# An order of loads and of weight conversions at the start of an attention and gated-network kernel

## Chip, cores, metric

One core of one Trainium2 chip. The metric is the device time of one launch in microseconds, as the median of several runs. The five engines are TensorE (PE, with its weight loads shown apart as PEld), VectorE (DVE), ScalarE (ACT), GpSimd (POOL) and SyncE (SP), whose queue here issues nearly all transfers. Each engine takes its instructions strictly in program order.

## What is computed

Three stages follow each other. First attention with a causal window: 4 sequences of 576 tokens, 8 heads of 64 columns, the first four heads with a window of 32 neighbours, the others with every fourth token of 128. Then a gated layer, and at last a soft mixture of 8 experts over all 2304 tokens.

```python
scores = np.where(masks[None], scale * np.matmul(q, k.transpose(0, 1, 3, 2)), -1e9)
attn = np.exp(scores - scores.max(-1, keepdims=True))
attn = attn / (attn.sum(-1, keepdims=True) + 1e-09)
x = np.matmul(attn, v)                      # to 2304 x 512
x = (1 / (1 + np.exp(-(x @ w_gate)))) * (x @ w_val) @ w_out      # 512 -> 1536 -> 512
logits = x @ phi                            # 32 slots
d, c = softmax(logits, 0), softmax(logits, 1)
slots = d.T @ x                             # 8 experts x 4 slots
out = c @ experts(slots, w1, w2)            # relu between w1 and w2
```

## The kernel before

**Work and its names.** Tokens are cut into five blocks, n = 0 to 4 (four of 512 tokens, one of 256). The attention of one block is four *units*, one for each pair of heads, so units 0 to 3 belong to block 0, units 4 and on to the next. A unit loads its queries and keys (`qk`, line 273, 528 or 576 KB) and its values (`v`, line 280, 512 KB). TensorE makes the scores (`s_ps`, line 162) on top of a mask (line 148); VectorE takes the maximum (`mx`, 176) and subtracts it (178); ScalarE takes the exponential (184); VectorE sums it (`su`, 186), adds 1e-9 (187), inverts (188) and scales (189; from unit 4 on GpSimd does the scaling). TensorE transposes the shares (`tr`, 195), ScalarE copies them out (`pt_ring`, 196), TensorE weights the values with them (`xp`, 222), 32 products that the hardware runs as 64 passes. The result is split into a high part (`x_hi`, ScalarE, 250) and a remainder (`x_lo`, VectorE, 251).

**Weight tiles.** The gate and value weights are twelve *tiles* f = 0 to 11 of 128 columns each. They come as doubles (`st`, line 365, 1 MB) and are *converted* to single precision by integer work in two halves of 512 columns (`convert`, from line 371): a ScalarE step (383), two VectorE steps (384, 385), one GpSimd step (386). The converted tile is stored to DRAM for later (`wg`, 369) and *split* into a high and a low part (`split_w`: ScalarE 437, VectorE 438). `l1` multiplies a tile with block 0: for each half (a = 0 gate, a = 1 value) twelve products of 512 columns (line 474) into one of two PSUM banks (`l1ps`). ScalarE's tanh (484) empties the bank of the first half, VectorE's gate (`gated`, 460) that of the second; the bank is then free for the half after the next.

**Order.** The order in the program is written by emission, and an instruction scheduler of the framework sorts TensorE, VectorE, ScalarE and GpSimd between the points that are pinned; loads in this part are pinned in the order in which they are emitted (`ld`). The start runs block 0's attention (`s_step`, `t_step`, `p_step`), and `head` is the call that issues the first weight tile's load. Within these steps, after step `C0`, tile 0's conversion, the loads of units 4 and 5, and tile 1's conversion are emitted (lines 889 to 897). The loop behind takes tile f's split, then the conversion of tile f + 2 (`LA`), then `l1`, with the attention of the next blocks spread between.

**Buffers.** Values of two units share a buffer and there are two of them, so those of units 4 and 5 wait until unit 1 is weighted. Staged doubles (`l2`) have two buffers: tile 2's load waits until tile 0 has been converted.

Of the kernel before, what the change touches and what calls it, by code (L numbers as in the profile page):

```python
# [39 lines left out]
def k_cols(n, hp):  # L40
    if n < 4:
        return 544 if hp < 2 else 640
    return 640 if hp < 2 else 1024
# [13 lines left out]
def tile_kernel(  # L57
# [25 lines left out]
    def b8(tag, shape, dt, name):  # L83
        return big.tile(shape, dt, tag=tag, name=name, bufs=BUFS[tag])
# [23 lines left out]
    def keep_warm(count):  # L108
        for _ in range(count):
            nc.tensor.matmul(idle, lhsT=zero[:, 0:P], rhs=zero[:, 512:1024], start=True, stop=True)  # L110
# [61 lines left out]
    def softmax(u, norm):  # L172
        s = u["s"].rearrange("p (a c) -> p a c", a=8)
        mx = sm.tile([P, 8], F32, tag="mx", name="mx")
        for r in range(2):
            nc.vector.tensor_reduce(mx[:, 4 * r : 4 * r + 4], u["s_ps"][r], AX.X, ALU.max)  # L176
        for r in range(2):
            nc.vector.tensor_tensor(
                s[:, 4 * r : 4 * r + 4],
                u["s_ps"][r],  # L180
                mx[:, 4 * r : 4 * r + 4].unsqueeze(2).to_broadcast([P, 4, 64]),
                ALU.subtract,
            )
        nc.scalar.activation(s, s, AF.Exp, scale=0.125)
        su = sm.tile([P, 8], F32, tag="su", name="su")
        nc.vector.tensor_reduce(su, s, AX.X, ALU.add)
        nc.vector.tensor_scalar(su, su, 1e-9, None, ALU.add)
        nc.vector.reciprocal(su, su)
        norm.tensor_tensor(s, s, su.unsqueeze(2).to_broadcast([P, 8, 64]), ALU.mult)
# [66 lines left out]
    def ld(ins):  # L256
        return tc.keep_in_program_order(ins) if early[0] else ins

    def attn_steps(pbs, norm, head=None):
        jobs = [(n, hp) for n in pbs for hp in HP_ORDER]  # L260
        us = [{"id": j, "z": z} for z, j in enumerate(jobs)]
        tags = ["qk", "qk", "gb", "gb"] if head else ["qk"] * len(jobs)

        def load_qk(z):
            n, hp = jobs[z]
            w = 512 + k_cols(n, hp)
            us[z]["qk"] = b8(tags[z], [P, 2048], F32, "qk")
            if n < 4:
                us[z]["s"], us[z]["slot"] = sm4[:, HP_ORDER.index(hp)], z % 4
            else:  # L270
                us[z]["s"] = pt_ring[:, 2 + z % 2].rearrange("p c i q -> p (c i q)")
                us[z]["slot"] = z % 2
            ld(nc.sync.dma_start(us[z]["qk"][:, 0:w], qkv[n * NHP + hp, :, VCOLS : VCOLS + w]))

        def load_v(z):
            n, hp = jobs[z]
            if z % 2 == 0:
                v2 = b8("v", [P, 2, VCOLS], F32, "v2")
                us[z]["v"], us[z + 1]["v"] = v2[:, 0], v2[:, 1]
            ld(nc.sync.dma_start(us[z]["v"], qkv[n * NHP + hp, :, 0:VCOLS]))  # L280

        def load(z, what):
            if z < len(us) and not head:
                what(z)

        begun = []

        def first(what):
            if what not in begun:
                begun.append(what)  # L290
                what(0)
                what(1)

        def s_step(z, ts=range(4)):
            if z == 0 and 0 in ts:
                if head:
                    load_qk(0)
                    ld(nc.sync.dma_start(msk, masks.bitcast(BF16)))
                    load_qk(1)
                    ld(nc.sync.dma_start(cst, consts))  # L300
                    load_v(0)
                    load_qk(2)
                    load_v(1)
                    head()
                    load_qk(3)
                    load_v(2)
                    load_v(3)
                else:
                    first(load_qk)
                    first(load_v)  # L310
            scores(us[z], ts)
            if 3 not in ts:
                return
            if 2 <= z and not head:
                weighted(us[z - 2], range(2), us[z])
            softmax(us[z], norm)
            load(z + 2, load_qk)
            if z == 0:
                load(2, load_v)

        def t_step(z):
            turn_unit(us[z])

        def p_step(z, ts=range(2)):
            if head or z + 2 >= len(us):
                weighted(us[z], ts)
            if head:
                keep_warm(WP)
            if 1 in ts:
                finish_unit(us[z])  # L330
                load(z + 3, load_v)

        def sp_step(z):
            if z < len(jobs):
                s_step(z)
            if z >= 2:
                p_step(z - 2)

        steps = []
        for z in range(len(jobs) + (1 if head else 2)):  # L340
            turned = [(t_step, z - 1)] if 0 < z <= len(jobs) else []
            if head:
                score = [(s_step, z, [t]) for t in range(4)] if z < len(jobs) else []
                steps += score + turned + ([(p_step, z - 1, [t]) for t in range(2)] if z else [])
            else:
                steps += [(sp_step, z)] + turned
        return steps, lambda: first(load_qk), lambda: first(load_v)
# [19 lines left out]
    def store():  # L367
        while stores:
            ld(nc.sync.dma_start(*stores.pop(0)))
# [63 lines left out]
    def split_w(src, pool=(True, False)):  # L433
        whl = b8("w", [P, 2, 2, ND, P], F32R, "whl")
        src = src.rearrange("p (a k c) -> p a k c", a=2, k=ND)
        for h in range(2):
            nc.scalar.copy(whl[:, 0, h], src[:, h])  # L437
            (nc.gpsimd if pool[h] else nc.vector).tensor_tensor(  # L438
                whl[:, 1, h], src[:, h], whl[:, 0, h].bitcast(F32), ALU.subtract
            )  # L440
        return whl
# [443 lines left out]
    def ahead(z):  # L885
        if z < NF:
            conv[z] = convert(z)

    for z, (fn, *args) in enumerate(attn_steps([0], nc.vector, lambda: stage(0))[0]):
        fn(*args)  # L890
        if z == C0:
            steps, first_qk, first_v = attn_steps([1, 2, 3, 4], nc.gpsimd)
            sab = Spread(steps, [(2 * NF - 2, 10), (4 * NF - 4, len(steps))])
            ahead(0)
            first_qk()
            ahead(1)
            first_v()

    def load_w(z):
# [4 lines left out]
    grouped[0] = True  # L904
    for f in range(NF):
        whl = split_w(conv.pop(f), SPL)
        ahead(f + LA)
        if f >= 10:
            store()
            load_w(f - 10)  # L910
        l1(0, f, whl, sab)
# [376 lines left out]
```

## Time and profile before

| What | Value |
|---|---|
| Median of 3 runs | 489.82 us (488.33 to 490.61) |
| The profiled execution's own time | 491.67 us |
| Its span | 489.9 us |
| TensorE busy | 467.3 us (95%) |
| VectorE, ScalarE, GpSimd busy | 309.0, 214.8, 155.0 us |
| Moved by DMA | 112.14 MB, 229 GB/s on average |

Times below are microseconds from the span's start. A row of the timeline begins with start and duration; behind the operation stand what it writes and reads and, after an x, how many instructions were merged into the row; brackets give the engine's idle time just before and what ended it. "issue" is a wait for which the profile shows no cause. In a row of windows each engine's busy time is followed by its number of instructions; then come the granted clock of TensorE, the share of time that the DMA engines were busy, and GB/s.

### The profile page before, as it was taken

The page shows a single profiled execution, that of the slowest core. Times are in us where ns is not written, and L with a number is a line of the kernel's source. Part 1 is how long each engine was busy: PE and PEld are TensorE (multiplying, and loading weights), DVE is VectorE, ACT ScalarE, POOL GpSimd, SP SyncE. Part 2 cuts the span into 40 slices and gives each one's busy share as a digit, 9 for nine tenths or more (in the row PEclk, how much of TensorE's full clock was granted, in tenths as well). Part 3 has the DMA queues.
Part 4 walks back from the last instruction along what each step waited for, and adds up shares of the span by engine and source line. Part 5 has one row for each costly group of instructions (what it writes and reads, how often), then busy time and mean ns, then how long its engine had stood idle before and what let it go on. Part 6 is the DMA issues. An engine that isn't in the chain of part 4 may idle for free.

```text
span 489.9 us, 12823 instructions
## 1 busy us (share of the span) xinstructions
PE 467.3 (95%) x5483; PEld 359.4 (73%) x5488; DVE 309.0 (63%) x629; ACT 214.8 (44%) x414; POOL 155.0 (32%) x132
## 2 busy tenths in 40 slices
PE   6789999999999999999999999999999999999993
PEld 3558888888787787786788888888787989642652
DVE  3878889849577666467776566566556665531532
ACT  2455555534456544444354545545434344200222
POOL 0244455514554663612033333242312134010100
PEclk9889999999999999999999999999999999989998
DMA  8978979985998792122220220220699894668966
GB/s 329 402 273 298 347 253 326 340 309 180 369 313 328 267 331 91 51 87 87 87 88 1 86 87 0 87 86 2 249 374 425 320 352 172 258 260 353 425 240 227
DMA packets 23785, 112.14 MB, mean 229 GB/s; under 512 B 2352, under 2 KB 7216, under 8 KB 14640
## 3 DMA queue, kind: packets, MB, share of 16 engines
q1 hardware_dynamic: 23408, 111.06, 61.2%
q8 instruction: 43, 0.70, 0.6%
q10 hardware_dynamic: 320, 0.26, 0.2%
q14 instruction: 14, 0.11, 0.1%
HBM read 97.16 MB, written 14.16 MB: 227 GB/s over the span
## 4 chain that ended last, share of the span: by engine, by line
PE 89%; DVE 3%; ACT 2%; issue 1%; DMA 1%; POOL 1%; SPq 0%; DVEq 0%; ACTq 0%; POOLq 0%
PE l1ps L474 33%; PE pa L596 13%; PE pe L596 6%; PE tp L761 4%; PE so_ps L1113 3%; PE pd L596 3%; PE s_ps L222 3%; PE h_ps L1054 3%; PE sp L790 3%; PE s_ps L162 3%; PE lt_ps L725 3%; PE tr L195 2%; DMA qk<-qkv 1%; PE wt_ps L412 1%; PE op L1152 1%
## 5 line engine op out<-in xcount | busy, mean ns | idle before, releaser
L474 PE MATMUL l1ps<-x_hi,whl 128*128 128x512 f32 x384 | 130.0, 404 | 1.8 <-ACT x_hi L250 1.8
L474 PEld LDWEIGHTS l1ps<-x_hi,whl 128*128 128x128 f32 x384 | 72.2, 189 | 17.5 <-ACT x_hi L250 2.3
L474 PE MATMUL l1ps<-x_lo,whl 128*128 128x512 f32 x192 | 76.0, 396 | 0.0
L386 POOL TENSOR_TENSOR fw<-fw 128x512 int32<-128x512 int32 x36 | 48.9, 1368 | 61.3 <-DVE fw L385 28.2
L474 PEld LDWEIGHTS l1ps<-x_lo,whl 128*128 128x128 f32 x192 | 36.5, 190 | 6.7 <-DVE x_lo L251 0.2
L460 DVE SCALAR_TENSOR_TENSOR g<-g,l1ps 128x512 f32<-128x512 f32 (+1 forms) x36 | 21.4, 594 | 29.3 <-PE l1ps L474 29.1
L474 PE MATMUL l1ps<-x,whl 128*128 128x256 f32 x288 | 37.0, 285 | 0.0
L474 PEld LDWEIGHTS l1ps<-x,whl 128*128 128x128 f32 x288 | 35.4, 192 | 0.4 <-issue 0.2
L484 ACT ACTIVATE g<-l1ps 128x512 f32<-128x512 f32 (+1 forms) x36 | 19.0, 526 | 36.8 <-PE l1ps L474 36.6
L438 POOL TENSOR_TENSOR whl<-w,whl 128x512 fp32r<-128x512 f32 x12 | 15.9, 1329 | 51.2 <-ACT whl L437 39.7
L761 PEld LDWEIGHTS tp<-cst,g 128*128 128x128 f32 x216 | 24.0, 140 | 5.6 <-issue 4.1
L761 PE MATMUL tp<-cst,g 128*128 128x128 f32 x216 | 27.9, 275 | 0.0
L383 ACT ACTIVATE fw<-st 128x512 f32<-128x512 f32 x36 | 22.9, 677 | 10.2 <-DMA st<-wd 10.2
L766 ACT COPY gt<-tp 128x512 f32<-128x512 f32 x27 | 15.8, 585 | 25.9 <-PE tp L761 21.7
L438 POOL TENSOR_TENSOR whl<-wst,whl 128x512 fp32r<-128x512 f32 x12 | 16.3, 1360 | 29.8 <-ACT whl L437 24.8
L659 DVE TENSOR_TENSOR tm<-pe,tm 128x512 f32<-128x512 f32 x12 | 8.3, 692 | 24.6 <-PE pe L596 24.6
L384 DVE TENSOR_SCALAR fw<-fw 128x512 uint32<-128x512 uint32 x36 | 22.6, 639 | 1.9 <-ACT fw L383 1.3
L176 DVE TENSOR_REDUCE mx<-s_ps 128x4 f32<-128x256 f32 x40 | 15.3, 413 | 11.8 <-PE s_ps L162 9.1
L438 DVE TENSOR_TENSOR whl<-fw,whl 128x512 fp32r<-128x512 f32 x24 | 20.4, 863 | 2.2 <-ACT whl L437 1.7
L385 DVE TENSOR_SCALAR fw<-st 128x512 int32<-128x512 uint32 x36 | 18.7, 548 | 4.5 <-DMA st<-wd 4.3
L437 ACT CAST whl<-fw 128x512 fp32r<-128x512 f32 x24 | 14.6, 620 | 14.7 <-POOL fw L386 8.2
L162 PE MATMUL s_ps<-qk 64*32 64x64 f32 x1280 | 17.7, 228 | 3.3 <-issue 2.2
(455 smaller groups left out, 953.8 us busy)
## 6 DMA issues: line engine op xcount, KB each, us to landing
ew<-w SPq DMA_DIRECT2D x32, 1024.0 KB, 7.4
st<-wd SPq DMA_DIRECT2D x18, 1024.0 KB, 9.3
wst<-wg SPq DMA_DIRECT2D x12, 1024.0 KB, 6.5
v<-qkv SPq DMA_DIRECT2D x20, 512.0 KB, 6.1
wg<-fw SPq DMA_DIRECT2D x12, 512.0 KB, 8.1
w<-wg SPq DMA_DIRECT2D x6, 1024.0 KB, 7.1
qk<-qkv SPq DMA_DIRECT2D x10, 576.0 KB, 5.0
qk<-qkv SPq DMA_DIRECT2D x8, 528.0 KB, 5.2
```

The lines of the kernel that those rows point to most:

```text
L162: nc.tensor.matmul(u["s_ps"][r][32 * i : 32 * i + 32, t, :], lhsT=q[64 * r : 64 * r + 64, 128 * t + 32 * i : 128 * t + 32 * i + 32], rhs=k ...
L383: nc.scalar.activation(top, st[:, c, 1].bitcast(F32), AF.Prelu, scale=2.0**-112, alpha=2.0**32)
L384: nc.vector.tensor_scalar(top.bitcast(U32), top.bitcast(U32), 3, None, ALU.logical_shift_left)
L385: nc.vector.tensor_scalar(low.bitcast(I32), st[:, c, 0], 2.0**-29, None, ALU.mult)
L386: nc.gpsimd.tensor_tensor(low.bitcast(I32), top.bitcast(I32), low.bitcast(I32), ALU.add)
L438: (nc.gpsimd if pool[h] else nc.vector).tensor_tensor(whl[:, 1, h], src[:, h], whl[:, 0, h].bitcast(F32), ALU.subtract)
L460: return nc.vector.scalar_tensor_tensor(g, g, 1.0, val, ALU.add, ALU.mult)
L474: nc.tensor.matmul(pt[:, 0:nt], lhsT=whl[:, w_, a, dc, :], rhs=x_[n][:, dc, :], start=first, stop=(dc == HP_ORDER[-1] and w_ == 1),)
L484: nc.scalar.activation(g, pt[:, 0:nt], AF.Tanh, scale=0.5)
L596: nc.tensor.matmul(pt, lhsT=w[:, w_, P * c : P * c + P], rhs=x_[:, c], start=first and c == 0 and w_ == 0 and x_ is hi, stop=c == 1 and w_ ...
L761: nc.tensor.transpose(tp[:, c], g_sb[self.n, 4 * q + c][:, P * j : P * j + P], ident)
L766: nc.scalar.copy(to, tp)
```

## The change

Two places. In the first block's attention the load of unit 3's queries and keys goes ahead of the first weight tile's load. And tile 1's conversion is no longer emitted between the loads for units 4 and 5, but in the loop, behind tile 0's split.

```diff
                     load_qk(2)
                     load_v(1)
+                    load_qk(3)
                     head()
-                    load_qk(3)
                     load_v(2)
                     load_v(3)
...
             ahead(0)
             first_qk()
-            ahead(1)
             first_v()
...
     for f in range(NF):
         whl = split_w(conv.pop(f), SPL)
+        if f == 0:
+            ahead(1)
         ahead(f + LA)
```

SyncE's queue, from the last load ahead of the change on (`v_179` holds the values of units 0 and 1, `v_188` those of 2 and 3, `v_500` before and `v_488` now those of 4 and 5):

```order
 L280 DMA v_179<-qkv 128x1024
+L273 DMA qk<-qkv 128x1152
 L365 DMA st<-wd 128x2048
-L273 DMA qk<-qkv 128x1152
 L280 DMA v_188<-qkv 128x1024 x2
 L365 DMA st<-wd 128x2048
 L273 DMA qk<-qkv 128x1056
 L273 DMA qk<-qkv 128x1152
+L280 DMA v_488<-qkv 128x1024 x2
 L365 DMA st<-wd 128x2048
 L369 DMA wg_0_81<-fw 128x1024
-L280 DMA v_500<-qkv 128x1024 x2
```

Unit 3's keys pass tile 0 (the first `st`); the values of units 4 and 5 pass tile 2 (the third `st`) and the store of tile 0.

VectorE at tile 0, before (`x_lo<-xp_291` and `xp_292` are unit 0's remainder):

```order
L385 TENSOR_SCALAR fw<-st 128x512 x2
L384 TENSOR_SCALAR fw<-fw 128x512
L186 TENSOR_REDUCE su<-sm_172 128x8
L438 TENSOR_TENSOR whl<-fw,whl 128x512
L251 TENSOR_TENSOR x_lo<-xp_291,x_hi 128x2x128
L251 TENSOR_TENSOR x_lo<-xp_292,x_hi 128x2x128
```

And now, from unit 1's remainder (`xp_386`, `xp_387`) to unit 2's (`xp_497`):

```order
L251 TENSOR_TENSOR x_lo<-xp_386,x_hi 128x2x128
L251 TENSOR_TENSOR x_lo<-xp_387,x_hi 128x2x128
L188 RECIPROCAL su<-su 128x8
L385 TENSOR_SCALAR fw<-st 128x512
L189 TENSOR_TENSOR sm_172<-sm_172,su 128x512
L438 TENSOR_TENSOR whl<-fw,whl 128x512
L384 TENSOR_SCALAR fw<-fw 128x512
L385 TENSOR_SCALAR fw<-st 128x512
L438 TENSOR_TENSOR whl<-fw,whl 128x512
L384 TENSOR_SCALAR fw<-fw 128x512
L251 TENSOR_TENSOR x_lo<-xp_497,x_hi 128x2x128
```

The last integer step of tile 0 (the first row of line 385 here) stood ahead of unit 0's remainder and now stands behind unit 1's; both steps of tile 1's first half come between the two halves of tile 0's split.

ScalarE around unit 3's high part, before (`xp_555`, `xp_556` are unit 3):

```order
L437 CAST whl<-fw 128x512
L196 COPY pt_ring<-tr 128x512
L383 ACTIVATE fw<-st 128x512
L250 CAST x_hi<-xp_555 128x2x128
L250 CAST x_hi<-xp_556 128x2x128
L383 ACTIVATE fw<-st 128x512
L484 ACTIVATE g<-l1ps 128x512
```

and now (`xp_543`, `xp_544` are unit 3):

```order
L437 CAST whl<-fw 128x512
L196 COPY pt_ring<-tr 128x512
L437 CAST whl<-fw 128x512
L250 CAST x_hi<-xp_543 128x2x128
L250 CAST x_hi<-xp_544 128x2x128
L484 ACTIVATE g<-l1ps 128x512
L383 ACTIVATE fw<-st 128x512 x2
```

The split's copy of tile 1's second half comes just ahead of unit 3's high part, and both steps on tile 2 move from around it to behind the first tanh.

## Rows read from the trace of the kernel before

**Rows 1.** The page: busy time of TensorE; the span in 40 slices, in tenths.

```profile
PE 467.3 (95%) x5483; PEld 359.4 (73%) x5488; DVE 309.0 (63%) x629; ACT 214.8 (44%) x414; POOL 155.0 (32%) x132
...
PE   6789999999999999999999999999999999999993
```

**Rows 2.** The chain of waits, 0 to 60 us: start, us, what.

```profile
10.19 2.19 issue
...
23.56 1.10 issue
...
34.52 0.64 ACT x_hi L250 x2
```

**Rows 3.** DMA queues (queue, packets, MB, share); TensorE between its two stops, by windows.

```profile
q8 instruction: 43, 0.70, 0.6%
...
12.37:18.66 6.29, 5.11 (x126) 3.41 (x127) 4.57 (x13) 2.51 (x5) 1.39 (x1) 0.73 1.03 422
18.66:24.66 6.00, 4.07 (x128) 3.02 (x127) 5.91 (x14) 2.84 (x6) 1.27 (x1) 1.00 1.01 382
```

**Rows 4.** SyncE's queue in order of time: start, us, line, transfer.

```profile
4.04 0.44 SPq L365 DMA_DIRECT2D st<-wd  x1
4.52 0.43 SPq L273 DMA_DIRECT2D qk<-qkv  x1
...
17.92 0.33 SPq L365 DMA_DIRECT2D st<-wd  x1
...
25.16 0.81 SPq L280 DMA_DIRECT2D v<-qkv  x2
```

**Rows 5.** DMA issues at 4.04, 4.52, 17.92 us: KB, us to landing.

```profile
st<-wd SPq DMA_DIRECT2D x1, 1024.0 KB, 11.0
...
qk<-qkv SPq DMA_DIRECT2D x1, 576.0 KB, 11.9
...
st<-wd SPq DMA_DIRECT2D x1, 1024.0 KB, 9.7
```

**Rows 6.** VectorE in order of time: start, us, line, operation.

```profile
16.58 0.75 DVE L385 TENSOR_SCALAR fw<-st 128x512 int32<-128x512 uint32 x2
...
25.53 0.76 DVE L251 TENSOR_TENSOR x_lo<-xp,x_hi 128x256 fp32r<-128x256 f32 x2 [0.76 <-ACT x_hi L250]
...
27.72 1.51 DVE L384 TENSOR_SCALAR fw<-fw 128x512 uint32<-128x512 uint32 x1
...
34.90 0.76 DVE L251 TENSOR_TENSOR x_lo<-xp,x_hi 128x256 fp32r<-128x256 f32 x2 [0.80 <-ACT x_hi L250]
...
40.71 0.68 DVE L186 TENSOR_REDUCE su<-sm 128x8 f32<-128x512 f32 x1
...
45.00 0.67 DVE L460 SCALAR_TENSOR_TENSOR g<-g,l1ps 128x512 f32<-128x512 f32 x1
...
47.05 0.68 DVE L438 TENSOR_TENSOR whl<-fw,whl 128x512 fp32r<-128x512 f32 x1
```

**Rows 7.** ScalarE in order of time.

```profile
32.97 0.68 ACT L383 ACTIVATE fw<-st 128x512 f32<-128x512 f32 x1
...
36.47 0.60 ACT L484 ACTIVATE g<-l1ps 128x512 f32<-128x512 f32 x1 [0.76 <-PE l1ps L474]
```

**Rows 8.** GpSimd in order of time.

```profile
29.64 1.80 POOL L386 TENSOR_TENSOR fw<-fw 128x512 int32<-128x512 int32 x1 [0.70 <-DVE fw L385]
34.18 1.27 POOL L386 TENSOR_TENSOR fw<-fw 128x512 int32<-128x512 int32 x1 [2.73 <-DVE fw L384]
```

**Rows 9.** TensorE in order of time.

```profile
24.67 0.42 PE L222 MATMUL xp<-pt_ring,v 64*64 64x32 f32 x13 [1.10 <-issue]
...
47.74 0.48 PE L474 MATMUL l1ps<-x_hi,whl 128*128 128x512 f32 x1
...
50.37 0.62 PE L474 MATMUL l1ps<-x_hi,whl 128*128 128x512 f32 x2
```

**Rows 10.** Windows of 12 us: busy time of the engines, 36 to 48 us.

```profile
36.00:48.00 12.00, 12.00 (x177) 9.37 (x177) 10.30 (x25) 6.24 (x11) 5.00 (x4) 1.00 0.78 269
```

## The prediction

> **What bounds the kernel now.** I read the page first: TensorE is busy for 467.3 of 489.9 us, and the slices show nine tenths or more everywhere but in the first three [rows 1]. So the body is paced by TensorE. An edit of the start can pay only with idle TensorE time before about 35 us, and can cost only by making TensorE wait behind it. Next I read the chain of waits of that start: it holds a stop of 2.19 us at 10.19, another of 1.10 us at 23.56, and last, at 34.52, ScalarE's copy of unit 3's result (x_hi), after which the gate products follow one another [rows 2]. The kernel's end moves with two things: when x_hi of unit 3 comes, and whether the conversions of weight tiles 1, 2, 3, ... keep their lead over TensorE after that.
>
> The two stops are called "issue": no semaphore stands behind them [rows 2]. The page's instruction queue brings 43 pieces in 0.70 MB, so 16 KB each, and TensorE's 10,971 instructions (products and weight loads) make 255 for each piece. Between the ends of the two stops TensorE took 126+127 and 128+127 instructions, in 6.29 and 6.00 us [rows 3]: a piece in each half. I read this as TensorE's own code arriving piece by piece, one in 6.0 to 6.3 us as long as the load queue is full (DMA share 1.03 and 1.01 there).
>
> **The change, part by part.** (1) *Keys of unit 3 ahead of weight tile 0.* Both transfers are issued half a microsecond apart [rows 4] and land 11.0 and 11.9 us later [rows 5]: the weights at 15.0, the keys at 16.4. Exchanged, the keys (576 KB, 1.4 us of the queue) land at about 14.0 and the weights at 16.4: 2.4 us gained by the scores of unit 3, 1.4 us lost by the first conversion. All loads behind keep their place.
>
> (2) *The earlier scores buy nothing before 24.7.* The new order lets TensorE take them before unit 0 is weighted, but the next pieces of code bar the way at 18.66 and 24.67. Before the change the second bar stood ahead of the last 13 of the 64 passes of unit 1's weighting [rows 9]. The change takes five gate products (ten instructions) out from in front, so it stands five passes later; eight passes, some 0.25 us, are left. Unit 1 is then weighted at about 24.95 instead of 25.1: a gain of 0.15 us.
>
> [...]
>
> (3) *Tile 0 is converted late, tile 1 behind its split.* That is the costly part. A half tile's conversion is one step on ScalarE (0.68, a tanh 0.60 [rows 7]), two integer steps on VectorE (two in 0.75 [rows 6]) and one on GpSimd (1.27 undisturbed, 1.80 beside VectorE [rows 8]); its split is a ScalarE copy (an estimate from the two: 0.62) and 0.68 on VectorE [rows 6]. Where VectorE meets GpSimd on such work it waits: 1.51 us for a step of 0.4 [rows 6]. Before, VectorE's two integer steps of tile 0 ran at 16.58 [rows 6]. Now the one of its second half stands behind unit 1's remainder (x_lo), which waits for 24.95. I follow the new orders of VectorE, ScalarE and GpSimd, once with 1.27 us and once with 1.80 us for GpSimd:
> - x_lo of unit 1 ends at 26.15 (26.29 less 0.15), the integer step at 26.65; GpSimd ends tile 0 at 27.9 or 28.45.
> - VectorE splits tile 0's first half behind it (+0.6) and does tile 1's two steps (+0.75); GpSimd has tile 1's first half at 30.5 or 31.6. VectorE's next step waits for that (+0.3), then x_lo of unit 2 and the last step (+1.05), then GpSimd: 33.1 or 34.75 (before 29.64+1.80 = 31.4).
> - ScalarE's copy of tile 1's second half stands ahead of x_hi of unit 3: +0.62, then +0.64, so x_hi ends at 34.4 or 36.05. Before it ended at 35.16. The gained 2.4 us are gone. x_lo of unit 3, behind one more split on VectorE, ends at 35.1 or 36.8, before 35.66 [rows 6]. TensorE's shift here: -0.55 or +1.15.
> - Tile 2: ScalarE's first step on it ran at 32.97, ahead of the first tanh at 36.47 [rows 7]; now it comes after the tanh, and VectorE's steps after the first gate. GpSimd begins tile 2 at 39.2 or 40.9 instead of 34.18 [rows 8]: 5.0 or 6.7 us late.
> - GpSimd's second half ends at 42.1 or 44.9; a ScalarE copy, a tanh and unit 4's exponential (1.85 together) bring VectorE's row sum of unit 4 to 44.0 or 46.8 instead of 40.71 [rows 6]. From that sum to the end of the second gate VectorE worked 4.96 us without a pause (40.71 to 45.67); two subtractions now come behind the gate, which leaves 4.2: the gate ends at 48.2 or 51.0. It frees the PSUM bank that TensorE wants for tile 2's second half, before at 47.74 [rows 9], a lead of 2.07 us; now at 47.2 or 48.9. TensorE waits 1.0 or 2.1.
> - Tile 3: split done at 47.73 [rows 6], used at 50.37 [rows 9], lead 2.64. VectorE is 3.3 or 6.1 late, TensorE 0.45 or 3.25: a wait of 0.2 in both.
>
> Sum: -0.55+1.0+0.2 = 0.65 us, or 1.15+2.1+0.2 = 3.45 us. I take the second: in this stretch the rows of tile 1, where both engines are at it, show 1.80 and 1.51 [rows 6, 8]. VectorE is busy for 10.30 of the 12 us from 36 to 48 [rows 10], so it can't work off 6 us of lateness soon, and I add 0.8 us for the tiles after (an estimate: one and a half more meetings at 1.80-1.27 = 0.53). Together 4.25 us.
>
> (4) *Values of units 4 and 5 ahead of tile 2's load.* Tile 2 was issued at 17.92, these values at 25.16 [rows 4]. Now both wait for unit 1's weighting, and the load comes third, at about 25.7. Before, the tile took 9.7 us from issue to landing with the queue full [rows 5]; as long again, it lands at 35.4. Its first reader, ScalarE, comes at 37.2 or later by the walk: nothing, with 1.8 us of cover at the least.
>
> **How the numbers follow.** The profiled execution took 491.67 us, 1.85 more than the median of 489.82 and 1.78 more than its own span. With 4.25 us it becomes 495.9, and the median of the runs 494.0. What a measurement of this kernel can tell from no change is 0.5%, 2.45 us: 487.4 to 492.3.
>
> *Forecast, 0.62: slower, 494.0, by itself 492.3 to 497.* The conversions lose their lead, TensorE waits for VectorE's gates. The upper end is the case where no lead covers anything any more: 6.7 us late.
>
> *Rival B, 0.25: the leads hold, 490.5.* If GpSimd and VectorE miss each other, the walk gives 0.65 us. For it: tile 2's row at 1.27 [rows 8]. Against: the row at 1.80 just before. That a change of the queue's order simply gets lost behind later work comes out here as well.
>
> *Rival C, 0.13: faster, 487.1.* The place is TensorE's code at 24.67. The whole walk hangs on that time: each microsecond that unit 1 is weighted sooner takes one off the sum, until the weights of tile 0 (16.4) bound it. If the piece is there when TensorE arrives, unit 1 is weighted at about 21.55 (an estimate: its weighting takes 1.0, and its scores and its transposes are ready before 20), 3.4 us sooner, and the quiet column gives 0.65-3.4 = -2.75. It decides from 3.1 us on. For it: in the change nothing is queued for a while before 25, and an emptier queue should pass code sooner. Against: the queue is as full as before up to about 22, and the contended column would stay slower, at 4.25-3.4 = 0.85.
>
> Slower takes 0.62, same 0.25, faster 0.13. The range 488.7 to 496.9 leaves out most of rival C and a tail of 0.05 above.
>
> **What would show it.** Right: the stop named "issue" on TensorE still ends at 24.3 to 24.8; GpSimd's first step on tile 0 after 22 us and on tile 2 after 39; x_hi of unit 3 between 34.4 and 36; after that new waits of TensorE for VectorE (its gate) between 45 and 75 us, 2 to 4 us in sum, where the trace of before has none. Wrong: x_hi of unit 3 before 33.5 with no wait behind it (rival C), or waits of under 1 us in that stretch (rival B). If VectorE's integer steps show 0.4 us beside GpSimd throughout, the mechanism of the sum is wrong, whatever the time.

## The result and the profile after

| What | Before | After |
|---|---|---|
| Median of 6 runs | 489.52 us (488.33 to 490.61) | 494.11 us (492.37 to 496.59) |
| Ratio | | 1.0092, 95% interval 1.0065 to 1.012 |
| The profiled execution's own time | 491.67 us | 496.59 us |
| Its span | 489.9 us | 494.8 us |

By the ratio the change costs 4.5 us (3.2 to 5.9 by its interval). The forecast was 494.0.

The page of the changed kernel, busy time and the slices of TensorE and of its clock, answering to [rows 1]:

```profile
PE 471.4 (95%) x5483; PEld 362.8 (73%) x5488; DVE 313.7 (63%) x629; ACT 214.0 (43%) x414; POOL 155.2 (31%) x132
...
PE   6699999999899999999999999999999999999993
...
PEclk9869999999899999999999999999999999989998
```

TensorE is busy for 4.1 us longer with the same 5483 products. Part of that is a lower clock: its second and third slices, 12.4 to 37.1 us, show 8 and 6 tenths (before 8 and 8).

TensorE in order of time (start, us, line, operation; in brackets idle time before and what ended it), answering to [rows 2, 9]:

```profile
17.77 0.30 PE L162 MATMUL s_ps<-qk 64*32 64x64 f32 x3 [2.05 <-issue]
...
20.11 1.11 PE L195 MATMUL tr<-cst,sm 128*128 128x128 f32 x4 [0.98 <-DVE x_lo L251]
21.89 2.17 PE L222 MATMUL xp<-pt_ring,v 64*64 64x32 f32 x64 [0.68 <-ACT pt_ring L196]
25.00 1.11 PE L195 MATMUL tr<-cst,sm 128*128 128x128 f32 x4 [0.94 <-DVE x_lo L251]
25.76 0.78 PE L474 MATMUL l1ps<-x_hi,whl 128*128 128x512 f32 x1
...
50.02 0.50 PE L474 MATMUL l1ps<-x_hi,whl 128*128 128x512 f32 x1 [0.80 <-DVE g L460]
...
70.41 0.50 PE L474 MATMUL l1ps<-x_hi,whl 128*128 128x512 f32 x1 [0.79 <-DVE g L460]
```

The stop for code now stands inside unit 3's scores (17.77). The first gate product comes at 25.7; before it came at 19.7:

```profile
19.72 0.51 PE L474 MATMUL l1ps<-x_hi,whl 128*128 128x512 f32 x1
```

Two new stops end with VectorE's gate (50.02, 70.41); before there was none.

VectorE, answering to [rows 6]:

```profile
18.04 0.76 DVE L176 TENSOR_REDUCE mx<-s_ps 128x4 f32<-128x256 f32 x2 [2.60 <-PE s_ps L162]
...
23.01 0.42 DVE L385 TENSOR_SCALAR fw<-st 128x512 int32<-128x512 uint32 x1
...
24.52 0.76 DVE L251 TENSOR_TENSOR x_lo<-xp,x_hi 128x256 fp32r<-128x256 f32 x2 [0.69 <-ACT x_hi L250]
...
25.30 0.38 DVE L385 TENSOR_SCALAR fw<-st 128x512 int32<-128x512 uint32 x1
...
41.09 1.51 DVE L385 TENSOR_SCALAR fw<-st 128x512 int32<-128x512 uint32 x1
...
43.19 2.15 DVE L438 TENSOR_TENSOR whl<-fw,whl 128x512 fp32r<-128x512 f32 x2
45.66 0.69 DVE L186 TENSOR_REDUCE su<-sm 128x8 f32<-128x512 f32 x1 [0.32 <-ACT sm L184]
...
47.12 1.58 DVE L384 TENSOR_SCALAR fw<-fw 128x512 uint32<-128x512 uint32 x2
48.63 0.74 DVE L176 TENSOR_REDUCE mx<-s_ps 128x4 f32<-128x256 f32 x2
49.30 0.67 DVE L460 SCALAR_TENSOR_TENSOR g<-g,l1ps 128x512 f32<-128x512 f32 x1
```

At 18.04 it has stood for 2.60 us in front of unit 3's maxima, with tile 0's steps queued behind (23.01, 25.30; before both at 16.58). Before, these maxima stood behind tile 0's steps and behind unit 0's remainder (20.58):

```profile
21.32 0.41 DVE L176 TENSOR_REDUCE mx<-s_ps 128x4 f32<-128x256 f32 x1
```

The second gate begins at 49.30, before at 45.00.

ScalarE and GpSimd, answering to [rows 7, 8]:

```profile
33.48 0.62 ACT L437 CAST whl<-fw 128x512 fp32r<-128x512 f32 x1
35.45 0.65 ACT L250 CAST x_hi<-xp 128x256 fp32r<-128x256 f32 x2 [1.34 <-PE xp L222]
37.48 0.60 ACT L484 ACTIVATE g<-l1ps 128x512 f32<-128x512 f32 x1 [1.38 <-PE l1ps L474]
37.98 1.22 ACT L383 ACTIVATE fw<-st 128x512 f32<-128x512 f32 x2
```

```profile
23.50 1.45 POOL L386 TENSOR_TENSOR fw<-fw 128x512 int32<-128x512 int32 x1 [23.06 <-DVE su L187]
...
31.74 1.65 POOL L386 TENSOR_TENSOR fw<-fw 128x512 int32<-128x512 int32 x1 [1.36 <-DVE fw L385]
40.92 1.40 POOL L386 TENSOR_TENSOR fw<-fw 128x512 int32<-128x512 int32 x1 [7.53 <-DVE fw L385]
42.68 1.28 POOL L386 TENSOR_TENSOR fw<-fw 128x512 int32<-128x512 int32 x1 [0.36 <-DVE fw L385]
```

Unit 3's high part ends at 36.10 (before 35.15), and what it waited for was TensorE, 1.34 us, not the split's copy just ahead of it. Tile 2 follows the first tanh and reaches GpSimd at 40.92 (before 34.18).

Transfers: the issues of the keys of unit 3, of tile 0 and of tile 2 (KB, us to landing), answering to [rows 5]. They were issued at 4.67, 5.37 and 25.74, so they land at 13.9, 16.4 and 33.5.

```profile
qk<-qkv SPq DMA_DIRECT2D x1, 576.0 KB, 9.3
...
st<-wd SPq DMA_DIRECT2D x1, 1024.0 KB, 11.0
...
st<-wd SPq DMA_DIRECT2D x1, 1024.0 KB, 7.8
```

Windows (busy time of PE, PEld, DVE, ACT, POOL with numbers of instructions; then granted clock, DMA share, GB/s), answering to [rows 10]:

```profile
26.00:32.00 6.00, 6.00 (x75) 4.50 (x75) 6.00 (x10) 3.63 (x7) 3.34 (x3) 0.50 1.00 324
32.00:38.00 6.00, 6.00 (x121) 4.63 (x122) 1.71 (x4) 2.27 (x6) 1.39 (x1) 0.85 0.88 315
...
48.00:60.00 12.00, 11.20 (x171) 8.78 (x170) 11.26 (x20) 6.34 (x12) 6.74 (x6) 1.00 0.74 274
60.00:72.00 12.00, 11.21 (x51) 8.90 (x51) 11.86 (x22) 6.12 (x13) 6.41 (x5) 1.00 0.99 360
```

From 26 to 38 us TensorE never stands still; until 33.81 it runs at the half level of its clock (0.50 granted in the window from 26, 0.85 on average in the one from 32). Between 48 and 72 it loses 0.80 and 0.79 us, while VectorE is busy for 11.3 and 11.9 of 12 us.

**Where the 4.5 us are.** I take the weight load with which each tile's first gate product begins. Tile 1 begins 1.24 us later than before (37.73, now 38.97), tile 6 3.52 us later (71.92, now 75.44). So the head costs 1.24 and the two gate waits 2.28, more than the idle time in brackets, since a product that does not wait begins before the last one's row ends (in the change one begins at 38.97, and the row ahead of it, 0.39 from 38.73, ends at 39.12).

This pair of traces has one more place. The change is 3.53 us late at a gate product at 125.23 and 5.83 us late at one at 137.10. Between them TensorE stands 1.80 us for code (before 1.10 us at the same instruction, at 127.80), and right behind that its clock is at half for 3.41 us, from 132.79 to 136.21, which it is not before:

```profile
132.04 0.36 PE L222 MATMUL s_ps<-pt_ring,v 64*64 64x32 f32 x9 [1.80 <-issue]
```

```profile
132.00:136.20 4.20, 4.16 (x19) 3.32 (x20) 3.37 (x7) 1.26 (x2) 1.91 (x2) 0.59 0.95 324
```

A second trace of the changed kernel (e5) has neither the stop nor the half clock there and is 2.15 us late at that product, so this place is not shown to belong to the change. Nor does the trace of before stand for its runs: 491.67 us lies 1.6 to 2.3 us above the medians that they gave beside the experiments.

### The profile page after: what moved, and what is told of

Its sections match the earlier page's. It is cut to its first block, busy times and chain, and to the rows that moved or that the text cites. A ratio compares the mean times of both kernels' runs of the same rounds, so it can differ in the third digit from the quotient of the medians.

```text
span 494.8 us, 12823 instructions
## 1 busy us (share of the span) xinstructions
PE 471.4 (95%) x5483; PEld 362.8 (73%) x5488; DVE 313.7 (63%) x629; ACT 214.0 (43%) x414; POOL 155.2 (31%) x132
## 4 chain that ended last, share of the span: by engine, by line
PE 79%; DVE 3%; ACT 2%; DMA 1%; issue 1%; POOL 1%; SPq 0%; DVEq 0%; ACTq 0%; POOLq 0%
PE l1ps L474 27%; PE pa L596 13%; PE pe L596 6%; PE tp L761 4%; PE so_ps L1114 3%; PE pd L596 3%; PE h_ps L1055 3%; PE sp L790 3%; PE lt_ps L725 3%; PE s_ps L222 3%; PE s_ps L162 2%; DMA qk<-qkv 1%; PE wt_ps L412 1%; PE op L1153 1%; PE tr L195 1%; DVE whl L438 1%
## 5 line engine op out<-in xcount | busy, mean ns | idle before, releaser
L474 PE MATMUL l1ps<-x_hi,whl 128*128 128x512 f32 x384 | 131.6, 410 | 1.6 <-DVE g L460 1.6
L474 PEld LDWEIGHTS l1ps<-x_hi,whl 128*128 128x128 f32 x384 | 73.9, 193 | 18.4 <-DVE g L460 2.2
L460 DVE SCALAR_TENSOR_TENSOR g<-g,l1ps 128x512 f32<-128x512 f32 (+1 forms) x36 | 21.4, 594 | 24.3 <-PE l1ps L474 24.3
L484 ACT ACTIVATE g<-l1ps 128x512 f32<-128x512 f32 (+1 forms) x36 | 18.9, 524 | 34.1 <-PE l1ps L474 34.1
L438 DVE TENSOR_TENSOR whl<-fw,whl 128x512 fp32r<-128x512 f32 x24 | 23.7, 989 | 7.8 <-ACT whl L437 6.8
L761 PE MATMUL tp<-cst,g 128*128 128x128 f32 x216 | 27.9, 275 | 0.0
L383 ACT ACTIVATE fw<-st 128x512 f32<-128x512 f32 x36 | 22.9, 669 | 4.9 <-DMA st<-wd 4.8
L438 POOL TENSOR_TENSOR whl<-wst,whl 128x512 fp32r<-128x512 f32 x12 | 16.4, 1363 | 27.3 <-ACT whl L437 22.3
L659 DVE TENSOR_TENSOR tm<-pe,tm 128x512 f32<-128x512 f32 x12 | 8.3, 692 | 24.6 <-PE pe L596 24.6
L385 DVE TENSOR_SCALAR fw<-st 128x512 int32<-128x512 uint32 x36 | 19.7, 567 | 5.8 <-DMA st<-wd 5.6
L176 DVE TENSOR_REDUCE mx<-s_ps 128x4 f32<-128x256 f32 x40 | 15.1, 415 | 12.9 <-PE s_ps L162 11.3
```

The lines of the kernel that those rows point to most:

```text
L383: nc.scalar.activation(top, st[:, c, 1].bitcast(F32), AF.Prelu, scale=2.0**-112, alpha=2.0**32)
L385: nc.vector.tensor_scalar(low.bitcast(I32), st[:, c, 0], 2.0**-29, None, ALU.mult)
L438: (nc.gpsimd if pool[h] else nc.vector).tensor_tensor(whl[:, 1, h], src[:, h], whl[:, 0, h].bitcast(F32), ALU.subtract)
L460: return nc.vector.scalar_tensor_tensor(g, g, 1.0, val, ALU.add, ALU.mult)
L474: nc.tensor.matmul(pt[:, 0:nt], lhsT=whl[:, w_, a, dc, :], rhs=x_[n][:, dc, :], start=first, stop=(dc == HP_ORDER[-1] and w_ == 1),)
L484: nc.scalar.activation(g, pt[:, 0:nt], AF.Tanh, scale=0.5)
```

## The experiments

All twelve runs at a glance. "Tile 1" is the begin of its first gate product, "1 to 6" the time from there to tile 6, "half" the time at half clock (0.50 granted) before 45 us. The last three columns come from one trace per kernel.

| Run | Median, us | Ratio (95%) | Tile 1 | 1 to 6 | Half |
|---|---|---|---|---|---|
| before | 489.36 to 490.08 in five groups | | 37.73 | 34.19 | 6.8 |
| the change | 494.11 | 1.0092 (1.0065 to 1.012) | 38.97 | 36.47 | 13.7 |
| e1 first edit alone | 491.33 | 1.0037 (1.0007 to 1.0067) | 38.39 | 34.21 | 10.2 |
| e2 second edit alone | 491.65 | 1.0050 (1.0032 to 1.0068) | 37.61 | 36.20 | 6.8 |
| e3 both, values behind tile 2 | 492.54 | 1.0050 (1.0030 to 1.0071) | 37.76 | 34.61 | 10.2 |
| e4 before, other warm-up | 489.97 | 1.0025 (0.9999 to 1.0052) | 38.31 | 34.26 | 10.2 |
| e5 the change again | 494.76 | 1.0106 (1.0080 to 1.0132) | 38.58 | 36.54 | 13.7 |
| e6 the change, more filler | 492.54 | 1.0064 (1.0042 to 1.0087) | 38.22 | 35.26 | 10.2 |
| e7 e3, more filler | 491.43 | 1.0040 (1.0015 to 1.0064) | 39.56 | 34.19 | 13.7 |
| e8 e1, more filler | 492.31 | 1.0063 (1.0040 to 1.0086) | 39.10 | 34.22 | 6.8 |
| e9 the change, tile 2 pinned | 493.31 | 1.0076 (1.0048 to 1.0105) | 38.06 | 36.16 | 10.2 |
| e10 e2, tile 2 pinned | 490.36 | 1.0010 (0.9983 to 1.0036) | 36.85 | 34.14 | 3.4 |
| e11 e1, tile 0's steps first | 491.88 | 1.0053 (1.0027 to 1.0080) | 38.14 | 34.21 | 6.8 |
| e12 the change, tile 0's steps first | 494.84 | 1.0103 (1.0078 to 1.0128) | 40.05 | 36.21 | 10.2 |

### The two edits apart: e1, e2, e3

e1 has the first hunk of the change alone, e2 the second alone. e3 has both, but `first_v()`, the loads of the values of units 4 and 5, moves into the loop with tile 1's conversion and so stays behind tile 2's load:

```diff
             first_qk()
-            ahead(1)
-            first_v()
...
+        if f == 0:
+            ahead(1)
+            first_v()
```

> Only the first edit: unit 3's keys ahead of tile 0's load; the conversions and the values of units 4 and 5 are emitted as before. Theory A (the sum on record: tile 0 and tile 1 are converted late because tile 1's conversion is emitted behind tile 0's split): without that edit nearly no loss, 489.5 to 490.5 us, no wait of TensorE for a gate. Theory B (tile 0's weights land 1.4 us later, and everything hangs on them): nearly the whole loss, 492.5 to 494 us. Theory C (the values of units 4 and 5 stand ahead of tile 2's load, so that tile 2's steps are sorted behind the first tanh): 489.5 to 490.5 us, x_hi of unit 3 at about 35, no wait for a gate.

> Only the second edit: tile 1's conversion is emitted behind tile 0's split, and with it the values of units 4 and 5 are loaded ahead of tile 2's weights; tile 0's load stays ahead of unit 3's keys. Theory A: 491 to 494 us, tile 1's GpSimd steps start over 1 us later than the 27.28 of before. Theory B: no loss, 489 to 490 us. Theory C: 492 to 494 us; tile 0 and tile 1 are converted as early as before (GpSimd at 17.1 and 27.3), tile 2's first GpSimd step comes at 38 to 41 instead of 34.18, and TensorE waits for a gate ahead of tile 2's second half.

> Both edits, but the values of units 4 and 5 are emitted behind tile 1's conversion, so that their loads stand behind tile 2's as before. Theory A: the loss stays, 493 to 495 us. Theory B: the loss stays, 492.5 to 494 us. Theory C: the waits for gates at tile 2 and tile 6 go; what is left is the later x_hi of unit 3 (about 1 us): 490 to 491.5 us, tile 2's first GpSimd step at 35 to 37.

Each edit costs by itself: 1.8 us the first (ratio 1.0037; 0.3 to 3.3 by its interval), 2.4 us the second (1.0050; 1.6 to 3.3), 4.3 together, and the change 4.5. Within these intervals they add up, at different places. e1 has no gate wait (1 to 6 takes 34.21 as before) and is 0.66 late at tile 1. e2 begins tile 1 as before, and loses 2.0 between tiles 1 and 6. In e2 TensorE's rows show the two waits, one for the gate, one for a split that stands in the same queue of VectorE:

```profile
48.53 0.50 PE L474 MATMUL l1ps<-x_hi,whl 128*128 128x512 f32 x1 [0.65 <-DVE g L460]
...
66.50 0.73 PE L474 MATMUL l1ps<-x_hi,whl 128*128 128x512 f32 x2 [0.77 <-DVE whl L438]
```

And ScalarE in e2, with tile 2 (L383) behind the first tanh (L484), before the other way round [rows 7]:

```profile
36.36 0.60 ACT L484 ACTIVATE g<-l1ps 128x512 f32<-128x512 f32 x1 [1.34 <-PE l1ps L474]
36.85 1.23 ACT L383 ACTIVATE fw<-st 128x512 f32<-128x512 f32 x2
```

With the values behind tile 2's load (e3) the scheduler puts tile 2 ahead of the tanh (36.27) again:

```profile
33.97 0.65 ACT L250 CAST x_hi<-xp 128x256 fp32r<-128x256 f32 x2
34.50 1.23 ACT L383 ACTIVATE fw<-st 128x512 f32<-128x512 f32 x2
```

The gate waits are gone (34.61). Its total is still 2.4 us above the kernel before, more than the 0.4 us that its trace is late at tile 6. e3 and the change differ in nothing but the place of `first_v()`, so the gate waits belong to the place of the values' loads, not to tile 1's conversion being emitted later. How the place of a load makes ScalarE late, by the transfer or by the order, e9 and e10 ask.

### The code stops: e4

> The kernel before with another warm-up of TensorE: instead of 8 large and 70 small products on zeros (156 instructions) 11 large ones (22), so 134 instructions fewer ahead of everything. If the stops called issue are TensorE's own code arriving in pieces of 256 instructions, they move 134 instructions on in the program: the first from the 9th pass of unit 2's scores to behind all of them, the third from unit 1's weighting to about unit 2's; unit 2's scores then end near 11 instead of 13.5 us, x_hi of unit 3 comes 1.5 to 2.5 us earlier, and the kernel takes 487 to 488.5 us. If they are waits for data or for the load queue, they stay at the same passes, and the time stays at 489 to 490 us.

```diff
-WARM = 8
-SMALL = 70
+WARM = 11
+SMALL = 0
```

The 70 small warm-up products (and as many weight loads) are left out, three large ones added: 134 instructions fewer. The stops of before came at TensorE's instructions 448, 959, 4031 and 5055 (its semaphore instructions counted along), all 191 or 192 above a multiple of 256. In e4 all four are gone from their places in the program, and one is left to see, at instruction 4543, again 191 above a multiple: 0.84 us from 144.64. (Instruction 448 comes at 14.88 there, behind a wait of 0.68 us for ScalarE's copy; before, that wait was 0.67 us.) So the stops go by the count of TensorE's own instructions. That they wait for code is read from the page's instruction queue: before, pieces of 16 KB begin there at 10.13, 22.28, 125.52 and 153.23 us, and the four stops end 2.2 to 2.5 us later (12.38, 24.67, 127.80, 155.69); in the change pieces at 9.46, 15.34 and 129.88, and stops that end at 11.82, 17.77 and 132.04. The time did not gain: unit 3 ran into other waits, and tile 1 began at 38.31.

### The changed kernel again, and filler products: e5, e6, e7, e8

e5 is the change unaltered. e6, e7 and e8 are the change, e3 and e1 with this edit, which doubles the filler products of 512 columns between the steps of the first block's attention and leaves out 8 small ones at the very start, so that the count of instructions stays:

```diff
-SMALL = 70
+SMALL = 62
...
-WP = 1
+WP = 2
```

> The changed kernel once more, unaltered, for a second trace. In its first trace TensorE ran at half clock from 20.15 to 33.81 us; the kernel of e3, whose TensorE, VectorE and ScalarE rows agree with it to 0.02 us up to 30.2 us, came back to full clock at 30.62, and the first products of tile 1 stand 1.2 us apart from there. Theory A (the sum on record: ScalarE's split copy ahead of x_hi of unit 3, and VectorE and GpSimd meeting, delay that x_hi): x_hi of unit 3 again ends at 36.0 to 36.2 and tile 1's products begin at 38.9 to 39.0, whatever the clock does. Theory D (the head's shift is TensorE's half clock alone): if the half clock ends at about 30.5 this time, x_hi of unit 3 ends at 34.5 to 34.8 and tile 1 begins at 37.7 to 37.9. Both: two waits of TensorE for VectorE's gate, 0.6 to 1.2 us each, at tile 2 and at tile 5, and 493 to 495 us in the median.

> The changed kernel with twice the filler products of 512 columns in the first block's attention (16 instead of 8; 8 of the small ones at the very start are taken away, so that TensorE's instruction count stays). Theory D: TensorE is less idle between 12 and 25 us, so the half-clock stretch is shorter than 13.65 us, unit 3 is weighted earlier, x_hi of unit 3 ends at 34.8 or sooner and tile 1 begins at 37.8 or sooner; the two gate waits stay, total 492 to 493. Theory A: the fillers change nothing that VectorE, ScalarE and GpSimd do: x_hi of unit 3 at 36, total 494. Neither expects the gate waits to go away (values of units 4 and 5 still stand ahead of tile 2's load).

> As e3 (both edits, but the values of units 4 and 5 behind tile 2's load), with the same filler products as e6. Theory D with the values as the cause of the gate waits: neither a half clock longer than 7 us nor a gate wait of over 0.3 us between 40 and 75 us; tile 1 begins at 37 to 37.7 and the span is 488 to 490, so the total is 489.5 to 491.5, no slower than the kernel before. Theory A: as e3, 492.5.

> The first edit alone (e1) with the same filler products as e6. In e1 the half clock ran from 21.6 to 28.5 and the total was 1.8 us above the kernel before. Theory D: a shorter stretch, the total 489.5 to 490.5. Theory B (tile 0's weights landing 1.4 us later set the start): as e1, 491.3, whatever the clock.

e5 confirms the gate waits (1.6 us in two, 1 to 6 takes 36.54), and lies between the theories in the head: half clock until 32.58, high part of unit 3 at 35.69, tile 1 at 38.58. What the clock does is seen best between the first trace of the change and e3: from 25.0 to 30.2 us TensorE's rows are the same to 0.02 us (ahead of that they differ by up to 1.3). Then e3 gets its full clock back at 30.62, the change at 33.81. Windows of e3:

```profile
26.00:32.00 6.00, 6.00 (x80) 4.68 (x80) 6.00 (x10) 3.68 (x8) 3.34 (x3) 0.62 0.80 292
32.00:38.00 6.00, 6.00 (x146) 4.24 (x145) 3.68 (x10) 3.44 (x7) 2.87 (x3) 1.00 1.01 395
```

The high part of unit 3 begins at 33.97 there and at 35.45 in the change, tile 1 at 37.76 and 38.97. The same instructions in the same order up to there, 3.2 us more of half clock, 1.5 us at x_hi and 1.2 us at tile 1. So the clock is what made x_hi late in the first trace. e5 lies between the two in all three: full clock from 32.58, x_hi from 35.04, tile 1 at 38.58. Why the clock came back sooner in the one trace than in the other, no run shows.

As an account of the whole head, theory D fell. e7 had the fillers and 13.7 us of half clock, e8 had 6.8 and a late tile 1 all the same (39.10): TensorE stood 1.52 us for code at 22.7 and then 1.27 us at 24.6, in front of a gate product that this order puts ahead of unit 2's transposes. In e6 the fillers also changed ScalarE's order (both copies of tile 0's split together), and with it the first gate wait, so that its 492.54 says nothing on the clock alone. Nor did more filler shorten the half clock throughout: 10.2 us for 13.7 in e6, 6.8 for 10.2 in e8, but 13.7 for 10.2 in e7. That less standing of TensorE shortens it was an estimate; these runs do not show it.

### Order or transfer: e9, e10

Both pin one order by hand, in the change (e9) and in the second edit alone (e10): ScalarE's steps on tile 2 ahead of the first tanh. The loads stay where the change puts them. (The edit adds lines to the file: what was line 385 is 387 in these two kernels, 460 is 462, 484 is 486.)

```diff
-            nc.scalar.activation(top, st[:, c, 1].bitcast(F32), AF.Prelu, scale=2.0**-112, alpha=2.0**32)
+            step = nc.scalar.activation(top, st[:, c, 1].bitcast(F32), AF.Prelu, scale=2.0**-112, alpha=2.0**32)
+            if z == 2:
+                kept(step)
...
-                    nc.scalar.activation(g, pt[:, 0:nt], AF.Tanh, scale=0.5)
+                    th = nc.scalar.activation(g, pt[:, 0:nt], AF.Tanh, scale=0.5)
+                    if n == 0 and f == 0:
+                        kept(th)
```

> The changed kernel with one order pinned by hand: ScalarE's two steps on tile 2 ahead of the first tanh, as before the change. The loads keep the order of the change (values of units 4 and 5 ahead of tile 2's load). Theory C1 (what costs is ScalarE's order: tile 2 begins behind the first tanh, and VectorE and GpSimd with it): GpSimd begins tile 2 at about 37 to 38 instead of 40.5 to 40.9, the second gate ends at 47 to 48 instead of 49.6 to 50.0, and both gate waits of TensorE (0.8 us each in the trace, 1.2 and 1.1 us of shift) fall to under 0.3 us; the shift at tile 6 against the kernel before is that of the head alone, 0.8 to 1.3 us, and the total is 491.5 to 493. Theory C2 (what costs is the transfer: tile 2's doubles land at 33.5 instead of 27.6, and later ones late behind them): ScalarE waits for the data, the gate waits stay above 0.5 us each, total 494 to 495.

> The second edit alone (as e2), with the same pin. In e2 the two gate waits gave a shift of 1.9 us at tile 6, and 2.4 us at the end. Theory C1: no gate wait of over 0.3 us, tile 6 begins at 71.7 to 72.5 (before 71.92), the total within 0.8 us of the kernel before. Theory C2: as e2, tile 6 at 73.8 and 1.9 us or more above the kernel before.

e10 decides it: ratio 1.0010 (0.9983 to 1.0036), tiles 1 to 6 in 34.14. Its ScalarE:

```profile
35.03 1.28 ACT L383 ACTIVATE fw<-st 128x512 f32<-128x512 f32 x2 [1.28 <-DMA st<-wd]
36.21 0.59 ACT L486 ACTIVATE g<-l1ps 128x512 f32<-128x512 f32 x1
```

Here tile 2 even waits for its transfer, 1.28 us, and nothing behind it is late. So the second edit's loss between tiles 1 and 6 comes with the order that the scheduler made, not with the later load. Two reservations: the pin made the scheduler shift a few of VectorE's instructions as well (its second gate begins at 45.13 instead of 47.80 in e2), and the head of e10 is 0.76 us ahead of that of e2 (half clock 3.4 us instead of 6.8), so the stretch from 1 to 6 is the evidence, not the median.

In the change (e9) the pin took one of the waits away and made the other one longer, 1.70 us in one. VectorE's rows of e9 show why:

```profile
37.58 0.76 DVE L176 TENSOR_REDUCE mx<-s_ps 128x4 f32<-128x256 f32 x2 [1.83 <-PE s_ps L162]
38.25 0.75 DVE L387 TENSOR_SCALAR fw<-st 128x512 int32<-128x512 uint32 x2
...
48.68 0.69 DVE L186 TENSOR_REDUCE su<-sm 128x8 f32<-128x512 f32 x1 [0.69 <-ACT sm L184]
49.29 0.68 DVE L462 SCALAR_TENSOR_TENSOR g<-g,l1ps 128x512 f32<-128x512 f32 x1
```

The scheduler, sorting anew, put tile 2's integer steps (38.25) behind unit 4's maxima and the second gate (49.29) behind unit 5's row sum, which waits for ScalarE's exponential. GpSimd began tile 2 at 39.41, not at 37 to 38. Theory C1 holds for the second edit; for both edits together it takes VectorE's order as well, and that one I did not pin.

### Tile 0 ahead in VectorE's queue: e11, e12

```diff
-            ahead(0)
+            with tc.high_priority(offset=HIP*2):
+                ahead(0)
```

> The first edit alone (as e1), with tile 0's conversion at a higher priority for the scheduler: its four integer steps on VectorE stand directly behind the maxima of unit 3, ahead of unit 0's remainder. In e1 and in the changed kernel VectorE stood still for 2.3 and 2.6 us for unit 3's scores, which wait for TensorE's code, with tile 0's steps queued behind; GpSimd began tile 0 at 22.8 and 23.5 (before 17.1), and the first gate product came at 25.7 (before 19.7). Theory H (the head loses because tile 0 is converted late, so that TensorE has no gate products to do in its waits before 25 us and has them left at the end): GpSimd begins tile 0 at 20 to 21, the first product comes at 22 to 24.2, 18 products instead of 10 stand ahead of unit 3's high part, tile 1's products begin at 36.8 to 37.8 (e1 38.39, before 37.73), and the total is 488.5 to 490.5, not slower than the kernel before. Rival H2 (unit 1 sets the start, not tile 0): the four steps, 1.5 us, delay unit 0's remainder and with it the transposes and the weighting of unit 1; tile 1 begins at 38.3 to 39.3, the total is 491 to 492.

> The changed kernel with the same priority for tile 0's conversion. ScalarE's steps on tile 2 still stand behind the first tanh. Theory H together with theory C1: tile 1's products begin at 37.0 to 37.8 (38.97 and 38.58 in the two traces of the changed kernel), the head's shift is gone, but TensorE still waits for VectorE's gate between 45 and 75 us, 0.5 to 1.8 us in sum, and the total is 490.5 to 492.5. Rival H2: tile 1 at 38.6 or later, the total 494 as in the changed kernel.

Theory H was right up to its last step. The first gate product comes at 22.38 and 23.18, and TensorE takes as many of them ahead of unit 3 as before the change. But nothing is gained. VectorE and TensorE in e11:

```profile
17.77 0.76 DVE L176 TENSOR_REDUCE mx<-s_ps 128x4 f32<-128x256 f32 x2 [2.46 <-PE s_ps L162]
...
20.04 1.49 DVE L385 TENSOR_SCALAR fw<-st 128x512 int32<-128x512 uint32 x1
21.45 0.74 DVE L251 TENSOR_TENSOR x_lo<-xp,x_hi 128x256 fp32r<-128x256 f32 x2
```

```profile
21.92 0.88 PE L195 MATMUL tr<-cst,sm 128*128 128x128 f32 x4 [3.06 <-DVE x_lo L251]
```

Unit 0's remainder comes at 21.45 instead of 19.4 to 19.6, and unit 1's transposes wait for it, 3.06 us instead of 0.98. The rival H2 had this, and its totals: 491.88 and 494.84 (tile 1 of e11, at 38.14, came a little ahead of its 38.3). VectorE has lost 2.3 to 2.6 us in front of unit 3's maxima, and whichever work is put first behind them, the other is late. No run puts tile 0's steps ahead of these maxima, into the time in which VectorE stands. In the change ScalarE's first step on tile 0 ends at 17.06, so the two steps of its first half, some 0.75 us, would have fitted in before 18.04 (an estimate: two such steps took 0.75 in [rows 6]). That test of this account is missing.

No version of the change beat the kernel before. The nearest is e10, which can't be told from it.

## Why the prediction was right

The time and the sign held; two of the terms were put on the wrong cause. That 494.0 came so close to 494.11 is luck: the head had the right size for a wrong reason, the gates were forecast 0.8 us too large, and about 1 us of what the medians differ by stands in no term of mine.

**The signs named beforehand.** Most came: GpSimd's first step on tile 0 at 23.50 and on tile 2 at 40.92, and an integer step of 1.51 us on VectorE; x_hi of unit 3 ended at 36.10, at the edge of the 34.4 to 36 that I gave. The gate waits add up to 1.59 us in both traces of the change, more than rival B's 1 us and less than my 2 to 4. One did not come: no stop for code ends at 24.3 to 24.8. The first trace has none there, unit 1's 64 passes standing in one row (21.89), and e5 has one that ends at 23.92.

**Part (1), the landings.** Right: 13.9 and 16.4, forecast 14.0 and 16.4.

**Part (2), the code bars.** Right in part. A bar still stands in front of unit 3's scores, and it ends at 17.77, after 2.05 us (forecast 18.66); code came in steps of 6 us again (stops that end at 11.82 and 17.77, and in e5 at 11.83, 17.78 and 23.92), but 0.7 to 0.9 us earlier than I took from the trace of before, and unit 1's high part begins at 24.11 instead of 24.95. What the part left out is who stands behind the instruction that waits at the bar. I saw that the earlier scores buy nothing. I did not see that their maxima, on VectorE, are sorted ahead of tile 0's integer steps and of unit 0's remainder, and hold them up for 2.60 us.

**Part (3), the head: +1.15 forecast, +1.24 and +0.85 in the two traces.** The size was right, the step wrong. That "ScalarE's copy of tile 1's second half stands ahead of x_hi of unit 3" cost nothing: x_hi waited 1.34 us for TensorE, and in e3, with the same order on all four engines up to there, it began at 33.97. Tile 0 was late as forecast (GpSimd ends it at 27.4, forecast 27.9 or 28.45), but as far as the trace shows that hurts by way of TensorE. Until 25.7 it has no gate product to take, and from 15.7 on it stands four times (2.05, 0.98, 0.68, 0.94 us); its clock is at half from 20.15 to 33.81 (before 6.8 us in two parts); and from 25.0 on it is busy without a gap and too slow. That the standing brought the half clock is my estimate from this order in time; no run shows it, since none holds the clock fixed. The clock was in none of my terms. e11 and e12 show that tile 0's lateness alone is not the cost, since curing it makes unit 1 late.

**Part (3), tile 2 and the gates.** GpSimd begins tile 2 at 40.92 (forecast 40.9), the row sum of unit 4 at 45.66 (46.8), the second gate ends at 49.97 (51.0): the contended column, less one microsecond, since GpSimd ran beside VectorE at 1.40 and 1.28 us there and not at 1.80, while VectorE's steps took 1.51 for 0.42, 2.15 for two of 0.68 and 1.58 for two in 0.75. TensorE's shift there: 1.20, forecast 2.1. The wait at tile 3 (0.2) did not come; instead a second one came behind tile 5, 1.1 us of shift, for which the sum had 0.8 as "the tiles after". Together 2.3, forecast 3.1.

**Part (4), the values ahead of tile 2's load, "nothing".** Right for the transfer: it landed at 33.5, 4.4 us ahead of its reader, and e10 shows that a later one does no harm. But the sentence takes the wrong part of the change for harmless. It is this move that made the scheduler put tile 2 behind the tanh, and so it carries the gate waits, 2.0 to 2.3 us (e2, e3, e10). The forecast's number was safe because I read ScalarE's new order as it stood.

**Rivals.** B (the leads hold) fell with the two waits. C (code in time) fell: unit 1 was weighted 0.8 us sooner than forecast, not 3.4.

**What stays open.** The medians give 4.6 and 4.7, the traces 3.5 and 3.2 at tile 6. The differences, 1.1 and 1.5 us, are about the half-width of the interval (1.35 us), and no more than what the profiled execution of before lies above its median, so the traces can't say whether a third cost exists. For e1 and e3, too, the ratios (1.8 and 2.4 us) give more than their traces show at tile 6 (0.7 and 0.4).

The granted clock of every run is on record and points the same way. Its median is 0.989 over 85 runs of the kernel before, 0.980 over 12 of the change, 0.982 in e1 and 0.981 in e3, but 0.990 in e2 and in e10. So the kernels with the first edit and the old filler ran with less clock in most of their runs, and those with the second edit alone did not. Among the 85 runs of before, 0.01 less clock went with 2.7 us more time (a straight line through them; correlation -0.59). By that line, an estimate, 0.009 is 2.4 us, the head's shift included; with the gate waits of 2.3 us that is 4.7, beside the 4.6 of the medians. It goes together, and is no proof of cause: e8, with the first edit and more filler, is at 0.989 and no faster than e1. Why the clock is lower with the first edit no run shows.

## What to carry to other kernels

An operand that arrives early is worth nothing if its consumer waits for something else (here unit 3's keys landed at 13.9 instead of 16.4 us, and the last of its scores still stood until 17.77); worse, its follow-up work may now be sorted ahead of other engines' work and hold that up (2.60 us on VectorE). Compare the order of every engine, not only of the one that was meant, and ask at each waiting instruction who is queued behind it. And a load that is moved may change the order of instructions that have nothing to do with it (tiles 1 to 6 took 36.20 us in e2 and, with the order pinned and the loads of e2, 34.14 in e10): before blaming the transfer, pin the order and keep the load where it is.

## What was unexpected of the hardware

**TensorE's code stops differ from run to run.** In the stretch from 125 to 160 us, where products of 32 columns follow one another, the stops called "issue" added up to between 0.3 us (e12) and 1.9 us (e3) in fourteen traces, with no relation to the edits that I can see. Traces from one run each can't show a difference of 1 us behind that place.

**A late half-clock stretch comes and goes.** In 6 of the 14 traces (before, the change, e1, e3, e5, e6) TensorE fell to the half level of its clock (0.50 granted) for 3.41 us somewhere between 431 and 440 us; in the others it did not. From one gate product, at 163 to 169 us, to the end of the span these six took 326.3 to 327.3 us, the other eight 324.9 to 325.5. Two windows of the same time, the kernel before and e10:

```profile
431.00:437.00 6.00, 5.73 (x31) 1.42 (x31) 0.98 (x2) 0.00 (x0) 0.38 (x1) 0.72 0.61 235
```

```profile
431.00:437.00 6.00, 5.77 (x46) 2.26 (x49) 1.28 (x4) 0.37 (x1) 1.06 (x1) 1.00 0.75 281
```

TensorE is busy in both for 5.7 to 5.8 of 6 us, at 0.72 of its clock in the one and at 1.00 in the other. What brings the stretch I can't say. One as long came at 132.79 in the first trace of the change and in no other.
